# First x of an attention kernel loaded plainly and turned on TensorE, a smaller first piece of wq, and 40 instead of 48 heads with k turned on TensorE

## The chip, the core and the metric

The kernel runs on one core of a Trainium2 chip. The time is the device time of one execution in microseconds (us). Executions of one kernel differ here, so every comparison below is between several executions of both kernels made in the same rounds on the same chip, except where a single execution is named as such.

## The reference

Two independent problems, A and B, have the same shapes; the result is the two outputs side by side. Everything is bf16.

```python
# B=16 batches, Sq=144, D=448, H=16 heads, Sk=512 cached keys, Dh=256
q = (x @ wq).reshape(B, Sq, H, Dh).transpose(0, 2, 1, 3)
scores = einsum("bhqd,bhkd->bhqk", q, k_cache) * Dh ** -0.5
p = softmax(scores)
o = einsum("bhqk,bhkd->bhqd", p, v_cache)
out = o.transpose(0, 2, 1, 3).reshape(B, Sq, H * Dh) @ wo      # for A and for B
```

## The kernel before

One *unit* is one head of one batch: 256 units in A (numbers 0 to 255), 256 in B (256 to 511). Unit U needs its 256 columns of q, its k transposed (kT) and its v.

TensorE (PE) runs one step per unit. In step i it computes Q of unit i+3, the scores S of unit i+2, the product PV and the ones-sum (the row sums of the softmax, by a matmul with ones) of unit i, and some pieces of the output projection OP that are ready. kT comes in one of two ways. For the first units k is loaded plainly ("natural") and turned by 8 transposes on PE, which cost PE time. For the rest the load itself transposes, which costs PE nothing but holds the DMA queue about 1.6 times as long for each byte (17.07 us for the 4.2 MB of `k3` below, 1.35 us for a plain 512 KB).

All loads are issued by SyncE (SP) on one queue, in an order that is written down as a string for the start of A (START) and for the passage from A to B (MID). The letters are: `n3` plain k of units 6 and 7 (512 KB), `v3` their v (512 KB), `q0` a part of wq, `o0` an eighth of wo (448 KB), `x0` the x of four batches, transposed by the load in two issues, and `k3` a transposing load of the kT of 16 units, 48 to 63 (4.2 MB). `v` and `n` share a ring of nine slots; kT has room for 32 units.

```python
LQ, LS, LT = 3, 2, 4                 # Q, S and transposes run this many units ahead of PV
KW, KR = 16, 32                      # units per transposing load, units of kT kept
NV, NXG = 9, 2
NNAT = 3 * KW // UV                  # UV = 2 units per plain load: 24 loads, 48 units natural
# ...
START = ("n0 q0 x0 n1 v0 n2 q1 v1 n3 q2 n4 v2 n5 v3 q3 n6 v4 n7 v5 n8 v6 o0 n9 v7 n10 v8 o1 n11 v9 n12 v10 o2 n13 "
         "v11 n14 v12 o3 n15 v13 x1 n16 v14 o4 n17 v15 n18 v16 o5 n19 v17 n20 v18 o6 n21 v19 n22 v20 o7 n23 v21 v22 "
         "k3")
MID = ("k16 v127 v128 q0 v129 v130 q1 v131 q2 q3 v132 k17 v133 v134 v135 v136 v137 o0 o1 v138 o2 v139 o3 v140 o4 v141 "
       "o5 v142 o6 o7 k18")
# ...
def t_load_x(XG):                    # four batches of x, transposed by the load
    # ...
        q.dma_start_transpose(xt_sb[:, 0:3, c0:c0 + XB * SQ], x[:, 0:384]).then_inc(sems["xt%d" % sl], 16)
        return q.dma_start_transpose(xt_sb[:, 3, c0:c0 + XB * SQ], x[:, 320:448]).then_inc(sems["xt%d" % sl], 16)

def t_load_k(W):                     # kT of 16 units, transposed by the load
    # ...
        return q.dma_start_transpose(kt_sb[:, :, sl * KW * 128:(sl + 1) * KW * 128], src).then_inc(
            sems["kt%d" % sl], 16)

def t_tr(U, k):                      # half of a natural k: 4 transposes on PE, then a copy to kt_sb
    # ...
        for c in range(4):
            a = (4 * k + c) * 128
            ins = t.transpose(tr_ps[k][:, c * 128:(c + 1) * 128], v_sb[:, sl, j, a:a + 128], ident)

def q_pair(U):                       # 2: Q of this head for two batches at once, 1: for one, 0: done already
    b, h = unit(U)[1:]
    if U < NNAT * UV:
        return 1
    if U < NNAT * UV + H and h % 2 == 0:
        return 1
    # ... pairs from here on
# ... the program's steps, after the loads that are due in step i:
    u = i + LT
    if 0 <= u < NNAT * UV: t_tr(u, 0)
    u = i + LQ
    if 0 <= u < NT and q_pair(u): t_q(u); t_evac_q(u)
    u = i + LS
    if 0 <= u < NT: t_s(u)
    # ... t_tr(i + LT, 1), t_pv(i), t_sum(i), pieces of the output projection
```

## Time and profile before

| | before |
|---|---|
| time, median of the first 3 runs | 1067.63 us (1065.14 to 1068.06) |
| execution that was profiled | 1063.18 us, faster than all three |
| PE busy | 1043.1 of 1061.4 us |

In the profile, "PE" is the matmul unit, and a wait is idle time of an engine with the thing that ended it behind an arrow.

The page of before, three of its lines: the span, the busy time of the engines, and the chain of work that ended last by engine.

```profile
span 1061.4 us, 32383 instructions
...
PE 1043.1 (98%) x12736; PEld 895.5 (84%) x12736; DVE 670.9 (63%) x2063; ACT 706.4 (67%) x2133; POOL 625.6 (59%) x1030
...
PE 97%; DMA 2%; SPq 1%; DVE 0%; issue 0%; ACT 0%; DVEq 0%
```

PE is the bound: 97% of the chain is its own work. What is left to win is PE's work itself and some 18 us of idle time. The list of PE's waits of before says where most of that is; the columns are the total in us, how often, and the longest one.

```profile
PE s_ps L972 <- DMA v_sb<-in_A_k_cache_dram: 6.1, 4, 4.7
PE qp_ps L1018 <- DMA xt_sb<-in_A_x_dram: 3.6, 1, 3.6
PE ot_ps L1097 <- DMA v_sb<-in_B_v_cache_dram: 3.0, 1, 3.0
```

Two of the three are at the start of A: natural k (line 972 is the transposes) and x (line 1018 is Q); the third is in B. The timeline of SP of before shows why: start and duration of each issue, in us.

```profile
2.44 3.57 SPq L922 DMA_TRANSPOSE xt_sb<-in_A_x_dram  x1
6.05 1.87 SPq L923 DMA_TRANSPOSE xt_sb<-in_A_x_dram  x1
7.97 0.59 SPq L953 DMA_DIRECT2D v_sb<-in_A_k_cache_dram  x1
...
84.66 1.30 SPq L953 DMA_DIRECT2D v_sb<-in_A_k_cache_dram  x1
88.93 0.37 SPq L945 DMA_DIRECT2D v_sb<-in_A_v_cache_dram  x1
...
95.01 19.81 SPq L932 DMA_TRANSPOSE kt_sb<-in_A_k_cache_dram  x1
```

The two issues of x hold SP from 2.4 to 7.9 us, and the second natural k waits behind them. The last line is `k3`, the first transposing load of k: it takes SP 19.8 us to issue.

The timeline of PE of before, at the start and where `k3` is first used; the wait stands in brackets.

```profile
9.96 1.12 PE L1018 MATMUL qp_ps<-xt_sb,wq_sb 128*128 128x144 bf16 x8 [3.57 <-DMA xt_sb<-in_A_x_dram]
...
12.39 0.58 PE L972 MATMUL s_ps<-qt_sb,v_sb 128*128 128x128 bf16 x4 [0.88 <-DMA v_sb<-in_A_k_cache_dram]
...
119.93 0.66 PE L1052 MATMUL s_ps<-qt_sb,kt_sb 128*128 128x144 bf16 x8
120.43 0.66 PE L1097 MATMUL ot_ps<-pt_sb,v_sb 128*128 128x144 bf16 x8
```

The S at 119.93 is that of unit 48, the first to read `k3`. It has no bracket: `k3` had *landed* (its last byte had arrived) at 116.94 us (landings here and below are worked out from the traces), with 3.0 us to spare. Eight matmuls of 144 columns follow each other in 0.50 us at full rate (119.93 to 120.43), and take 0.96 us at half rate.

The table of stretches of before: stretch, length, busy time (and count) of PE, PEld, DVE, ACT and POOL, granted PE clock, DMA share, GB/s.

```profile
0.00:10.00 10.00, 1.66 (x13) 1.18 (x14) 2.67 (x4) 2.08 (x3) 0.70 (x6) 1.00 0.90 208
110.00:120.00 10.00, 10.00 (x137) 8.89 (x136) 6.81 (x26) 6.48 (x20) 5.48 (x10) 1.00 1.19 258
120.00:130.00 10.00, 10.00 (x127) 8.69 (x126) 6.75 (x20) 5.82 (x18) 5.00 (x9) 1.00 1.12 339
```

PE is nearly idle in the first ten microseconds and full around 120 us. But the queue has hardly a pause either: from 4.55 us to about 85 us, loads land one straight after another. There is one slack stretch, from about 85 to 98 us: SP waits there for PE to free a slot of `v` and `n` (nothing is issued between 85.96 and 88.93 us, see the timeline of SP), and landings come up to 2.6 us apart where 1.35 us is usual. The Trainium skill, "DMA: Bandwidth & Descriptors", section "Queues, rings and completion order", says that each DMA engine consumes descriptors in ring order; the trace agrees: in before all 86 transfers issued in the first 150 us land in the order of their issue.

### The profile page before, as it was taken

The numbers are of one execution on the slowest core, as the hardware profiler recorded it, in microseconds if no ns is written. First come the engines' busy times: TensorE is split into PE (matmuls) and PEld (weight loads), VectorE is DVE, ScalarE is ACT, GpSimd is POOL, SyncE is SP. The second block draws the span as 40 slices with busy tenths as digits, with TensorE's granted clock in tenths as the row PEclk, the third lists the DMA queues.
The fourth block names the chain that finished last, engine by engine and source line by source line (L and its number), as shares of the span: only waits on it lengthen the run. The fifth ranks groups of instructions, "written<-read, shape, count | busy, mean of one in ns | idle before, by whom it ended". The sixth has DMA issues, their size and how long they took to land.

```text
span 1061.4 us, 32383 instructions
## 1 busy us (share of the span) xinstructions
PE 1043.1 (98%) x12736; PEld 895.5 (84%) x12736; DVE 670.9 (63%) x2063; ACT 706.4 (67%) x2133; POOL 625.6 (59%) x1030
## 2 busy tenths in 40 slices
PE   6999999999999999999998999999999999999997
PEld 6999888888888888888887888888888888888885
DVE  4776666666666666666665666666666666666664
ACT  4887656667756666666855666676775666667674
POOL 3554555656656566666754656566665555666663
PEclk9999999999999999999998999999999999999999
DMA  9999999999999999999999999999999999999950
GB/s 304 379 350 285 295 293 254 274 297 273 292 276 298 208 280 267 290 292 298 262 287 352 265 274 290 291 290 301 264 263 265 304 285 289 289 290 279 239 187 13
DMA packets 588801, 294.15 MB, mean 277 GB/s; under 512 B 500576, under 2 KB 513376, under 8 KB 588640
## 3 DMA queue, kind: packets, MB, share of 16 engines
q1 hardware_dynamic: 588640, 291.99, 109.1%
q8 instruction: 102, 1.67, 0.6%
q14 instruction: 59, 0.48, 0.2%
HBM read 161.48 MB, written 4.13 MB: 156 GB/s over the span
## 4 chain that ended last, share of the span: by engine, by line
PE 97%; DMA 2%; SPq 1%; DVE 0%; issue 0%; ACT 0%; DVEq 0%
PE s_ps L1052 24%; PE ot_ps L1097 24%; PE qp_ps L1018 24%; PE op_ps L1196 20%; PE ot_ps L1109 3%; DMA v_sb<-in_A_k_cache_dram 1%; PE s_ps L972 1%; PE qp_ps L972 1%; PE qp_ps L1196 1%; DMA v_sb<-in_B_v_cache_dram 1%; SPq L922 0%; SPq L923 0%; DVE ost_sb L1217 0%; SPq L902 0%; DVE run_sb L1154 0%
## 5 line engine op out<-in xcount | busy, mean ns | idle before, releaser
L1072 POOL TENSOR_TENSOR pp_sb<-pt_sb 128x288 f32<-128x288 bf16 x512 | 374.0, 731 | 345.7 <-ACT pt_sb L1062 323.5
L1062 ACT ACTIVATE pt_sb<-s_ps 128x288 bf16<-128x288 f32 x1024 | 364.4, 408 | 268.5 <-PE s_ps L1052 268.0
L1154 DVE TENSOR_REDUCE run_sb<-ot_ps 1x1 bf16<-1x144 f32 x1024 | 262.3, 293 | 324.0 <-ACT rinv_sb L1120 324.0
L1097 PE MATMUL ot_ps<-pt_sb,v_sb 128*128 128x144 bf16 x4096 | 340.7, 226 | 3.0 <-DMA v_sb<-in_B_v_cache_dram 3.0
L1052 PE MATMUL s_ps<-qt_sb,kt_sb 128*128 128x144 bf16 x4096 | 340.8, 226 | 0.0
L1052 PEld LDWEIGHTS s_ps<-qt_sb,kt_sb 128*128 128x128 bf16 x4096 | 288.2, 98 | 43.5 <-DVE qt_sb L1032 0.2
L1018 PE MATMUL qp_ps<-xt_sb,wq_sb 128*128 128x288 bf16 (+1 forms) x2496 | 305.3, 266 | 3.6 <-DMA xt_sb<-in_A_x_dram 3.6
L1076 POOL TENSOR_TENSOR ps_sb<-pp_sb 128x144 bf16<-128x144 f32 x512 | 250.8, 490 | 76.2 <-PE ot_ps L1109 3.1
L1018 PEld LDWEIGHTS qp_ps<-xt_sb,wq_sb 128*128 128x128 bf16 x2496 | 218.8, 98 | 79.0 <-issue 4.4
L1196 PE MATMUL op_ps<-wo_sb,ring 128*128 128x448 bf16 x1120 | 285.0, 353 | 0.4 <-DVE ring L1140 0.4
L1097 PEld LDWEIGHTS ot_ps<-pt_sb,v_sb 128*128 128x128 bf16 x4096 | 274.6, 98 | 3.7 <-DMA v_sb<-in_B_v_cache_dram 3.2
L1140 DVE TENSOR_TENSOR ring<-ot_ps,rinv_sb 128x288 bf16<-128x288 f32 (+2 forms) x640 | 231.0, 375 | 0.0
L1120 ACT ACTIVATE rinv_sb<-ot_ps 128x144 f32<-128x144 f32 x512 | 150.1, 293 | 51.0 <-PE ot_ps L1109 8.0
L1032 DVE CAST qt_sb<-qp_ps 128x576 bf16<-128x576 f32 x200 | 151.1, 755 | 41.7 <-PE qp_ps L1018 37.6
L1125 ACT ACTIVATE rinv_sb<-rinv_sb 128x144 f32<-128x144 f32 x512 | 165.4, 323 | 16.1
L1109 PE MATMUL ot_ps<-ps_sb,ones 128*128 128x144 bf16 x512 | 115.9, 226 | 0.0
L1196 PEld LDWEIGHTS op_ps<-wo_sb,ring 128*128 128x128 bf16 x1120 | 94.0, 98 | 21.8 <-DVE ring L1140 0.8
L1031 DVE CAST qt_sb<-qp_ps 128x288 bf16<-128x288 f32 x112 | 49.2, 439 | 9.4 <-PE qp_ps L1018 8.8
L1109 PEld LDWEIGHTS ot_ps<-ps_sb,ones 128*128 128x128 bf16 x512 | 50.2, 98 | 0.0
L980 ACT ACTIVATE kt_sb<-qp_ps 128x512 bf16<-128x512 bf16 x48 | 28.9, 603 | 8.5 <-PE qp_ps L972 8.5
L972 PE MATMUL s_ps<-qt_sb,v_sb 128*128 128x128 bf16 x192 | 19.4, 226 | 6.2 <-DMA v_sb<-in_A_k_cache_dram 6.1
L980 DVE COPY kt_sb<-s_ps 128x512 bf16<-128x512 bf16 x48 | 19.5, 405 | 6.3 <-PE s_ps L972 6.2
(21 smaller groups left out, 85.1 us busy)
## 6 DMA issues: line engine op xcount, KB each, us to landing
v_sb<-in_A_v_cache_dram SPq DMA_DIRECT2D x128, 512.0 KB, 6.9
v_sb<-in_B_v_cache_dram SPq DMA_DIRECT2D x128, 512.0 KB, 7.1
v_sb<-in_A_k_cache_dram SPq DMA_DIRECT2D x24, 512.0 KB, 9.3
out_dram<-ost_sb SPq DMA_DIRECT2D x36, 112.0 KB, 6.1
wo_sb<-in_A_wo_dram SPq DMA_DIRECT2D x8, 448.0 KB, 8.5
wo_sb<-in_B_wo_dram SPq DMA_DIRECT2D x8, 448.0 KB, 8.9
wq_sb<-in_A_wq_dram SPq DMA_DIRECT2D x4, 768.0 KB, 9.2
wq_sb<-in_B_wq_dram SPq DMA_DIRECT2D x4, 768.0 KB, 10.1
```

Source lines behind the costliest of these rows:

```text
L1018: ins = t.matmul(acc, lhsT=wq_sb[:, kc, c0:c0 + 128], rhs=xt_sb[:, kc, xo:xo + n * SQ], start=(kc == 0), stop=(kc == 3))
L1032: return v.tensor_copy(qt_sb[:, a:b + 1:b - a, :, :], qp_ps[:, :, 0:2 * SQ].rearrange("p e (u q) -> p u e q", u=2))
L1052: ins = t.matmul(s_ps[bank][:, (c % 2) * SQ:(c % 2 + 1) * SQ], lhsT=kt_sb[:, 2 * c + dc, ko:ko + 128], rhs=qt_sb[:, qsl, dc, :], start=(dc ...
L1062: return a.activation(pt_sb[:, psl, 2 * k:2 * k + 2, :].rearrange("p b q -> p (b q)"), s_ps[bank][:, 0:2 * SQ], AF.Exp, scale=DH ** -0.5)
L1072: return g.tensor_tensor(pp_sb[:, :, :], pt_sb[:, psl, 0:2, :], pt_sb[:, psl, 2:4, :], op=ALU.add)
L1076: return g.tensor_tensor(ps_sb[:, sl, :], pp_sb[:, 0, :], pp_sb[:, 1, :], op=ALU.add)
L1097: ins = t.matmul(ot_ps[ob][:, dc * SQ:(dc + 1) * SQ], lhsT=v_sb[:, vsl, j, c * DH + dc * 128:c * DH + (dc + 1) * 128], rhs=pt_sb[:, sl, c, ...
L1109: return t.matmul(ot_ps[ob][:, 2 * SQ:3 * SQ], lhsT=ones[:, :], rhs=ps_sb[:, sl, :], start=True, stop=True)
L1125: return a.activation(rinv_sb[:, sl, :], ln, AF.Exp, scale=-1.0)
L1140: ins = v.tensor_tensor(ring[:, 2 * h:2 * h + 2, r0:r0 + q1 - q0], ot_ps[ob][:, 0:2 * SQ].rearrange("p (c q) -> p c q", c=2)[:, :, q0:q1], ...
L1154: return v.tensor_reduce(run_sb[0:1, k, j:j + 1], ot_ps[ob][0:1, 2 * SQ:3 * SQ], axis=AX.X, op=op)
L1196: ins = t.matmul(acc[0:m, 0:D], lhsT=ring[:, c, col0:col0 + m], rhs=wo_sb[:, c, :], start=(c == first), stop=(c == last))
```

## The change

The intent is to shorten the start and to take work off PE. x of batch 0 is loaded plainly and turned on PE, which waits there anyway. The first quarter of wq comes in two parts so that the first Q can start after one. The transposing `x0` (which still holds batch 0 to 3) is moved behind `v6`, and `x1` to the end. Units 40 to 47 no longer take 64 transposes on PE: a transposing load of 8 units (`k40.8`) brings their kT, and `k48.16` is the old `k3`.

```diff
-    NNAT = 3 * KW // UV
+    KO, Q1 = 8, 3
+    NNAT = 20
+    WQ_PARTS = (((0, 2), (2, 4)) + tuple((h, h + 4) for h in range(4, H, 4)), tuple((h, h + 4) for h in range(0, H, 4)))
@@
-    START = ("n0 q0 x0 n1 v0 n2 q1 v1 n3 q2 n4 v2 n5 v3 q3 n6 v4 n7 v5 n8 v6 o0 n9 v7 n10 v8 o1 n11 v9 n12 v10 o2 n13 "
-             "v11 n14 v12 o3 n15 v13 x1 n16 v14 o4 n17 v15 n18 v16 o5 n19 v17 n20 v18 o6 n21 v19 n22 v20 o7 n23 v21 v22 "
-             "k3")
+    START = ("n0 q0 n1 q1 v0 n2 q2 v1 n3 n4 v2 q3 n5 v3 n6 v4 q4 n7 v5 n8 v6 x0 n9 v7 n10 v8 o0 n11 v9 n12 v10 o1 n13 "
+             "v11 n14 v12 o2 n15 v13 o3 n16 v14 o4 n17 v15 n18 v16 o5 n19 v17 k40.8 v18 o6 v19 v20 o7 v21 v22 k48.16 v23 "
+             "v24 v25 x1")
@@ MID names its loads by first unit and count (k256.16 for k16), and is otherwise as before
@@
+        def t_load_xb():
+            def e(q):
+                q.dma_start(ost_sb[:, 0, :], A_x[0, 0:128, :]).then_inc(sems["xb"], 16)
+                return q.dma_start(ost_sb[0:SQ - 128, 1, :], A_x[0, 128:SQ, :]).then_inc(sems["xb"], 16)
+        def t_first_x():
+            def e(t):
+                for kc, d0 in enumerate((0, 128, 256, D - 128)):
+                    c0 = kc * SQ
+                    t.transpose(xb_ps[:, c0:c0 + 128], ost_sb[:, 0, d0:d0 + 128], ident)
+                    ins = t.transpose(xb_ps[:, c0 + 128:c0 + SQ], ost_sb[0:SQ - 128, 1, d0:d0 + 128], ...)
+            # then one DVE copy into the free second slot of xt_sb
@@ t_load_k(W) becomes t_load_k(u0, n): n = 8 or 16 units; two semaphores, one per 16 units of room
@@ def q_pair(U):
-            if U < NNAT * UV:
+            if b < Q1 and U < NU:
                 return 1
-            if U < NNAT * UV + H and h % 2 == 0:
+            if b == Q1 and U < NU and h % 2 == 0 and Q1 % 2:
                 return 1
@@
-            return 1 if j in (0, NXG * XB - 1) else (2 if j % 2 else 0)
+            if j in (0, NXG * XB - 1) or U // H in (XB - 1, XB):
+                return 1
+            return 2 if j % 2 else 0
```

Cut: the keys of wq and kT in the scheduler, and the parsing of the strings. The last part has a consequence: `x1` is now too late for pairs across batches 3 and 4, so the Q of units 49 to 63 are all single and those of 65 to 79 are no longer done ahead. There are 192 pairs and 128 single Q in place of 200 and 112.

More of the change, by code (lines that the diff above doesn't have):

```diff
@@ L806, in bass_concat_heads__mha_block_cached__gqa_block_cached__near_ridge_kernel @@
     LIM_EXP = 40
-    START = ("n0 q0 x0 n1 v0 n2 q1 v1 n3 q2 n4 v2 n5 v3 q3 n6 v4 n7 v5 n8 v6 o0 n9 v7 n10 v8 o1 n11 v9 n12 v10 o2 n13 "
-             "v11 n14 v12 o3 n15 v13 x1 n16 v14 o4 n17 v15 n18 v16 o5 n19 v17 n20 v18 o6 n21 v19 n22 v20 o7 n23 v21 v22 "
-             "k3")
-    MID = ("k16 v127 v128 q0 v129 v130 q1 v131 q2 q3 v132 k17 v133 v134 v135 v136 v137 o0 o1 v138 o2 v139 o3 v140 o4 v141 "
-           "o5 v142 o6 o7 k18")
+    START = ("n0 q0 n1 q1 v0 n2 q2 v1 n3 n4 v2 q3 n5 v3 n6 v4 q4 n7 v5 n8 v6 x0 n9 v7 n10 v8 o0 n11 v9 n12 v10 o1 n13 "
+             "v11 n14 v12 o2 n15 v13 o3 n16 v14 o4 n17 v15 n18 v16 o5 n19 v17 k40.8 v18 o6 v19 v20 o7 v21 v22 k48.16 v23 "
+             "v24 v25 x1")
+    MID = ("k256.16 v127 v128 q0 v129 v130 q1 v131 q2 q3 v132 k272.16 v133 v134 v135 v136 v137 o0 o1 v138 o2 v139 o3 v140 "
+           "o4 v141 o5 v142 o6 o7 k288.16")
     of = out.rearrange("b q e -> (b q) e")
@@ L847, in bass_concat_heads__mha_block_cached__gqa_block_cached__near_ridge_kernel @@
         tr_ps = (s_ps[2][:, :].bitcast(BF16), qp_ps[:, 1, :].bitcast(BF16))
+        xb_ps = op_ps[:, :].bitcast(BF16)
         ident = qt_sb[:, NQT - 1, 0, 0:128]
@@ L858, in bass_concat_heads__mha_block_cached__gqa_block_cached__near_ridge_kernel @@
             sem_names.append("xt%d" % i)
-        for i in range(HG):
+        for i in range(H // 2):
             sem_names.append("wq%d" % i)
+        sem_names.append("xb")
         for i in range(NWG):
@@ L893, in t_init, with t_load_wq @@
             S.add(POOL, e5, reads=[("ones", 0)], writes=[id_key], name="ident")
-        def t_load_wq(pr, hg):
-            cols = slice(hg * 4 * DH, (hg + 1) * 4 * DH)
+        def t_load_wq(pr, k):
+            h0, h1 = WQ_PARTS[pr][k]
+            cols = slice(h0 * DH, h1 * DH)
+            sem = "wq%d" % (h0 // 2)
             w = wqs[pr]
@@ L900, in e @@
                 q.dma_start(wq_sb[:, 0:3, cols], w[0:384, cols].rearrange("(c p) n -> p c n", p=128)).then_inc(
-                    sems["wq%d" % hg], 16)
-                return q.dma_start(wq_sb[64:128, 3, cols], w[384:448, cols]).then_inc(sems["wq%d" % hg], 16)
-            S.add(SP, e, writes=[(("wq", hg), pr)], dma_sem="wq%d" % hg, n_dma=2, name="wq%d.%d" % (pr, hg))
+                    sems[sem], 16)
+                return q.dma_start(wq_sb[64:128, 3, cols], w[384:448, cols]).then_inc(sems[sem], 16)
+            S.add(SP, e, writes=[(("wq", j), pr) for j in range(h0 // 2, h1 // 2)], dma_sem=sem, n_dma=2,
+                  name="wq%d.%d" % (pr, k))
         def t_load_wo(pr, wg):
@@ L924, in t_load_x, with ev, t_load_k @@
             S.add(SP, e, writes=[(("xt", sl), XG)], dma_sem="xt%d" % sl, n_dma=2, name="x%d" % XG)
-        def t_load_k(W):
-            pr, r0 = divmod(KW * W, NU)
-            sl = W % (KR // KW)
-            src = ks[pr].rearrange("b h (p c) d -> (b h p) (c d)", c=4)[r0 * 128:(r0 + KW) * 128, :]
+        def t_load_xb():
             def e(q):
-                return q.dma_start_transpose(kt_sb[:, :, sl * KW * 128:(sl + 1) * KW * 128], src).then_inc(
-                    sems["kt%d" % sl], 16)
-            S.add(SP, e, writes=[(("kt", sl), W)], dma_sem="kt%d" % sl, name="k%d" % W)
+                q.dma_start(ost_sb[:, 0, :], A_x[0, 0:128, :]).then_inc(sems["xb"], 16)
+                return q.dma_start(ost_sb[0:SQ - 128, 1, :], A_x[0, 128:SQ, :]).then_inc(sems["xb"], 16)
+            S.add(SP, e, writes=[(("ost", 0), -1), (("ost", 1), -1)], dma_sem="xb", n_dma=2, name="xb")
+        def t_first_x():
+            def e(t):
+                ins = None
+                for kc, d0 in enumerate((0, 128, 256, D - 128)):
+                    c0 = kc * SQ
+                    t.transpose(xb_ps[:, c0:c0 + 128], ost_sb[:, 0, d0:d0 + 128], ident)
+                    ins = t.transpose(xb_ps[:, c0 + 128:c0 + SQ], ost_sb[0:SQ - 128, 1, d0:d0 + 128],
+                                      ident[0:SQ - 128, 0:SQ - 128])
+                return ins
+            S.add(PE, e, reads=[(("ost", 0), -1), (("ost", 1), -1), id_key], writes=[("opp", "x")], banks=["op"],
+                  name="TX")
+            def ev(v):
+                return v.tensor_copy(xt_sb[:, :, XB * SQ:(XB + 1) * SQ],
+                                     xb_ps[:, 0:4 * SQ].rearrange("p (k q) -> p k q", k=4))
+            S.add(DVE, ev, reads=[("opp", "x")], writes=[(("xt", 1), -1)], banks=["op"], name="etx")
+        def t_load_k(u0, n):
+            pr, r0 = divmod(u0, NU)
+            c0 = u0 % KR * 128
+            sem = "kt%d" % (u0 % KR // KW)
+            src = ks[pr].rearrange("b h (p c) d -> (b h p) (c d)", c=4)[r0 * 128:(r0 + n) * 128, :]
+            def e(q):
+                return q.dma_start_transpose(kt_sb[:, :, c0:c0 + n * 128], src).then_inc(sems[sem], 16)
+            S.add(SP, e, writes=[(("kt", o % (KR // KO)), o) for o in range(u0 // KO, (u0 + n) // KO)], dma_sem=sem,
+                  name="k%d.%d" % (u0, n))
         def v_source(t, G):
@@ L959, in t_tr @@
             ko = U % KR * 128
-            kt_key = ("kt", U // KW % (KR // KW))
-            if k == 0 and U % KW == 0:
+            kt_key = ("kt", U // KO % (KR // KO))
+            if k == 0 and U % KO == 0:
                 S.res[kt_key] = _Res()
-                S.res[kt_key].version = U // KW
+                S.res[kt_key].version = U // KO
             bank, eng = (("s2", DVE), ("qp1", ACT))[k]
@@ L1008, in t_q @@
             xo = b % (NXG * XB) * SQ
-            xr = sorted(set((pr * Bn + b + k) // XB for k in range(n)))
-            hg = h // 4
+            xr = [(("xt", XG % NXG), XG) for XG in sorted(set((pr * Bn + b + k) // XB for k in range(n)))]
+            if U < H:
+                xo, xr = XB * SQ, [(("xt", 1), -1)]
             def e(t):
@@ L1020, in e @@
                 return ins
-            S.add(PE, e, reads=[(("wq", hg), pr), ("wqz", 0)] + [(("xt", XG % NXG), XG) for XG in xr],
+            S.add(PE, e, reads=[(("wq", h // 2), pr), ("wqz", 0)] + xr,
                   writes=[(bk, ("q", U)) for bk in q_banks[:n]], banks=q_banks[:n], name="Q%d" % U)
@@ L1038, in t_s @@
         def t_s(U):
-            W = U // KW
-            ksl = W % (KR // KW)
+            W = U // KO
+            ksl = W % (KR // KO)
             ko = U % KR * 128
@@ L1229, in bass_concat_heads__mha_block_cached__gqa_block_cached__near_ridge_kernel @@
         t_init()
+        t_load_xb()
+        t_first_x()
         s_min = -LQ - 24
@@ L1241, in bass_concat_heads__mha_block_cached__gqa_block_cached__near_ridge_kernel @@
             plan(lo, 0, t_load_x, XG)
-        for W in range(NNAT * UV // KW, NKW):
-            plan(KW * (W + 1) - KR - LS, 1, t_load_k, W)
+        for W in range(NKW):
+            plan(KW * (W + 1) - KR - LS, 1, t_load_k, KW * W, KW)
         table = {"x": t_load_x, "q": t_load_wq, "o": t_load_wo, "k": t_load_k, "n": t_load_n, "v": t_load_v}
-        start, mid = ([(table[w[0]], ((pr,) if w[0] in "qo" else ()) + (int(w[1:]),)) for w in tab.split()]
-                      for pr, tab in enumerate((START, MID)))
+        start, mid = ([(table[w[0]], ((pr,) if w[0] in "qo" else ()) + tuple(int(k) for k in w[1:].split(".") if k))
+                       for w in tab.split()] for pr, tab in enumerate((START, MID)))
         dma_plan = list(start)
+        k_first = sum(args[1] for fn, args in start if fn is t_load_k) + NNAT * UV
         for G in range(NVG):
@@ L1254, in bass_concat_heads__mha_block_cached__gqa_block_cached__near_ridge_kernel @@
                 dma_plan.extend(mid)
-            if (fn, args) in dma_plan:
+            if (fn, args) in dma_plan or fn is t_load_k and args[0] < k_first:
                 continue
@@ L1271, in bass_concat_heads__mha_block_cached__gqa_block_cached__near_ridge_kernel @@
             elif fn is t_load_k:
-                lo = KW * (args[0] + 1) - KR - LS
+                lo = sum(args) - KR - LS
             elif fn is t_load_x and args[0] >= NXG:
```

## The prediction

> **What bounds the kernel now.** TensorE: the page gives PE 1043.1 of 1061.4 us busy, the chain of waits 97% PE, and the busy table by 10 us stretches shows PE full from 40 us on. The loss lies at the start: PE is busy 1.66 us in 0-10 us. The list of waits has 4.7 us for the first natural k, 3.6 us for the transposing load of x, then 1 us for the second natural k, and the timeline shows matmul groups at half rate (8 in 0.96 us) until 16.4 us, then full rate (0.50 us). The queue's timeline says why: the two x transposes hold it from 2.44 to 7.92 us. The queue is the second bound: from 10 to 60 us it moves 362-388 GB/s. Landings, from the trace: 1.34 us for each 512 KB plain load, 3.2 us for a wq quarter, 17 us for a 16-unit transposing k load (4.2 MB, 246 GB/s; the Trainium skill, "DMA: Bandwidth & Descriptors", Latency and other measured facts, has 261 GB/s for one kernel: roughly agreed).
>
> **What the change does.**
> 1. x of batch 0 comes plainly (129 KB, two issues of 0.5 us) and is turned by 8 transposes on a cold PE that waits anyway; the first Q waits for half a quarter of wq. Estimates: first natural k lands at 5.6 us instead of 4.6, first Q at 7.3 instead of 9.96, second natural k at 8.6 instead of 12.3, that of unit 12 at 28.8 instead of 33.9.
> 2. The x transposes are deferred, not removed: behind v6 they cost the queue about 3.6 us. I put their landing at 42.3 us; unit 16's Q wants them at about 41.6. So the 5 us gained early shrinks to about 2.2 us: the start is bound by the queue's bytes, and those are nearly the same.
> 3. 8 natural units fewer: 64 transposes at 4 in 0.22 us, 3.6 us less PE work, all on the critical path. Against it 8 paired Q become 16 single ones: 0.98 against 2 x 0.50 us, 0.2 us more.
> 4. The k load for units 40-47 takes 8.5 us of queue where plain loads took 5.4; the second x group leaves this stretch. Estimate: the load for units 48-63 lands at about 113.5 us (116.9 before), while PE wants it at about 114 (119.93 before, 3.0 us to spare). A stall of 0-2 us, 0.4 expected. Later k loads in the first problem have 9 to 15 us to spare. The second problem and the tail do not change.
>
> Sum: -2.2 -3.6 +0.2 +0.4 = about -5.3 us, 0.5%.
>
> **Prediction: 1062.3 us** (from 1067.6), range 1057.5 to 1066. Faster by over 2%: 1%; within 2%: 98%; slower by over 2%: 1%.
>
> **What would show it.** Right: 320 natural transposes on PE, not 384; first Q at about 7 us, full rate from about 15 us; a new PE wait of about 1 us for the x transposes near 42 us; PE at 60 us only 2-3 us ahead of before; from 120 us on 5-6 us ahead, constant to the end. Wrong: a lead at 60 us of 5 us or more, or a wait of over 2 us on the transposing k load near 100-115 us, or waits at units 64-80.
>
> **What would make it wrong.** The half-quarter of wq with 1 KB rows may move slower; the clock may rise later, as PE waits more between groups; the x transposes may hide in the queue's backlog, giving 2-3 us more; the k load may come later and give the 3.6 us back; and executions spread by half of the effect (1065.1 to 1068.1).

## The result

| | before | after |
|---|---|---|
| runs of the comparison, median | 1066.6 us (4 runs) | 1067.99 us (1067.58 to 1068.65, 4 runs) |
| ratio of after to before | | 1.0014 (0.9996 to 1.0031) |
| profiled execution | 1063.18 us | 1067.58 us |

A ratio here and below is the mean time of one kernel's fast runs over that of the other's fast runs of the same rounds, so it is not quite the ratio of the medians quoted; the bracket is its 95% interval. The time is the same within 2%, and it lies above the range that was predicted. There was no gain at all.

The page of after, the same three lines.

```profile
span 1065.6 us, 32388 instructions
...
PE 1042.7 (98%) x12744; PEld 894.3 (84%) x12744; DVE 669.2 (63%) x2064; ACT 703.8 (66%) x2125; POOL 624.5 (59%) x1030
...
PE 93%; DMA 4%; SPq 3%; DVE 0%; issue 0%; ACT 0%; DVEq 0%
```

PE's own part of the chain fell from 97% to 93%. PE's count rises by 8 (64 transposes fewer, 8 for x, 64 because 8 pairs of Q became 16 single ones). Its busy time falls by only 0.4 us, though the trade should save about 3 us: part of the work ran slower, as will be seen. The list of PE's waits of after:

```profile
PE ot_ps L1132 <- DMA v_sb<-in_B_v_cache_dram: 4.8, 2, 2.9
PE op_ps L945 <- DMA ost_sb<-in_A_x_dram: 3.1, 1, 3.1
PE s_ps L1087 <- DMA kt_sb<-in_A_k_cache_dram: 2.9, 1, 2.9
PE s_ps L1004 <- DMA v_sb<-in_A_k_cache_dram: 2.2, 4, 0.9
...
PE qp_ps L1053 <- DMA wq_sb<-in_A_wq_dram: 1.1, 3, 0.4
PE ot_ps L1132 <- DMA v_sb<-in_A_v_cache_dram: 0.9, 1, 0.9
```

The wait of Q for x (3.6 us) is gone and that for natural k fell from 6.1 to 2.2 us. The 3.1 us of the second line are only the time until the plain x has landed, at the very start, and the 1.1 us are for parts of wq. The first line lies in B, to which experiments come back. Two waits in the middle of A are new: 2.9 us for a transposing load of k, and 0.9 us for a v. The timeline of SP of after:

```profile
28.85 9.27 SPq L929 DMA_TRANSPOSE xt_sb<-in_A_x_dram  x1
...
72.96 14.08 SPq L964 DMA_TRANSPOSE kt_sb<-in_A_k_cache_dram  x1
...
91.60 23.80 SPq L964 DMA_TRANSPOSE kt_sb<-in_A_k_cache_dram  x1
```

These are `x0`, `k40.8` and `k48.16`. The timeline of PE of after, at the start and around the new waits:

```profile
7.50 1.14 PE L1053 MATMUL qp_ps<-xt_sb,wq_sb 128*128 128x144 bf16 x8 [0.29 <-DMA wq_sb<-in_A_wq_dram]
...
9.52 0.59 PE L1004 MATMUL s_ps<-qt_sb,v_sb 128*128 128x128 bf16 x4 [0.46 <-DMA v_sb<-in_A_k_cache_dram]
...
114.51 0.66 PE L1053 MATMUL qp_ps<-xt_sb,wq_sb 128*128 128x144 bf16 x8
118.09 0.67 PE L1087 MATMUL s_ps<-qt_sb,kt_sb 128*128 128x144 bf16 x8 [2.92 <-DMA kt_sb<-in_A_k_cache_dram]
119.66 1.14 PE L1132 MATMUL ot_ps<-pt_sb,v_sb 128*128 128x144 bf16 x8 [0.89 <-DMA v_sb<-in_A_v_cache_dram]
120.59 0.33 PE L1144 MATMUL ot_ps<-ps_sb,ones 128*128 128x144 bf16 x1
120.71 1.70 PE L1231 MATMUL op_ps<-wo_sb,ring 128*128 128x448 bf16 x4
122.20 0.97 PE L1053 MATMUL qp_ps<-xt_sb,wq_sb 128*128 128x144 bf16 x8
123.01 0.66 PE L1087 MATMUL s_ps<-qt_sb,kt_sb 128*128 128x144 bf16 x8
```

PE has done its Q at 115.0 us, and waits until `k48.16` lands at 118.05. It runs one S, waits again for the v that landed behind `k48.16` at 119.61, and then does PV, the sum, four pieces of OP and much of a Q at about half rate: the PV takes 0.93 us to the next line, not 0.50. The stretch from the Q at 114.51 to the S at 123.01 is 8.50 us long. At full rate its work is Q 0.50, S 0.50, PV 0.50, sum 0.06, four pieces 0.76 and Q 0.50, that is 2.82 us, with durations of the same groups in before's timeline. So 5.68 us are lost: 3.8 in waits, 0.3 in the ends of the two groups before the waits (which the next group otherwise covers), and 1.5 in half-rate work (119.66 to 123.01 us, 3.35 us, for work that takes 1.82). The page counts the last two as busy.

The table of stretches of after:

```profile
0.00:10.00 10.00, 5.09 (x37) 3.74 (x38) 3.59 (x6) 2.68 (x4) 0.70 (x6) 1.00 0.75 247
110.00:120.00 10.00, 6.19 (x79) 5.12 (x77) 4.00 (x15) 3.98 (x12) 4.31 (x7) 0.97 1.23 258
120.00:130.00 10.00, 10.00 (x119) 8.56 (x118) 5.18 (x18) 5.30 (x16) 4.21 (x8) 0.86 1.14 313
```

In 110 to 120 us PE is busy for 6.19 us, and in 120 to 130 the clock is 0.86. The stretch from 120 to 130 looks full, but is not at full speed.

A *lead* makes this additive: by how much earlier than in the first profile of before the PV of a unit starts. Leads are worked out from the PE records of the traces, each of one execution, some of them on another chip.

| unit | 8 | 14 | 28 | 44 | 48 | 96 | 250 | 320 | 511 |
|---|---|---|---|---|---|---|---|---|---|
| start of its PV in before, us | 35.5 | 47.5 | 75.7 | 116.1 | 125.2 | 226.2 | 527.9 | 678.0 | 1050.5 |
| lead of after, us | 2.20 | 1.30 | 1.30 | 4.44 | -0.29 | -1.51 | -1.51 | -4.00 | -4.00 |

The start gains 1.30 us, the missing transposes 3.14, and between units 44 and 96 all of it and 1.5 us more is lost. (Read from 44 to 96 and not between: the other order of the Q alone moves the lead up and down by some 3 us there, as in half_wo below, where nothing waits: 6.06, 8.90 and 5.80 at units 44, 64 and 80.) Then nothing moves until B begins, where another 2.5 us go. The loss in A fits the ratio: +1.5 us is 0.14%. What B adds is against a lucky execution, as experiments show below.

### The profile page after: what moved, and what is told of

It reads as the page before. It is cut to its first block, busy times and chain, and to the rows that moved or that the text cites. A ratio compares the mean times of both kernels' runs of the same rounds, so it can differ in the third digit from the quotient of the medians.

```text
span 1065.6 us, 32388 instructions
## 1 busy us (share of the span) xinstructions
PE 1042.7 (98%) x12744; PEld 894.3 (84%) x12744; DVE 669.2 (63%) x2064; ACT 703.8 (66%) x2125; POOL 624.5 (59%) x1030
## 4 chain that ended last, share of the span: by engine, by line
PE 93%; DMA 4%; SPq 3%; DVE 0%; issue 0%; ACT 0%; DVEq 0%
PE ot_ps L1132 23%; PE s_ps L1087 23%; PE qp_ps L1053 23%; PE op_ps L1231 19%; PE ot_ps L1144 3%; SPq L964 2%; DMA wq_sb<-in_A_wq_dram 1%; DMA v_sb<-in_A_k_cache_dram 1%; DMA v_sb<-in_B_v_cache_dram 1%; PE s_ps L1004 1%; PE qp_ps L1004 1%; PE qp_ps L1231 1%; DMA v_sb<-in_A_v_cache_dram 0%; SPq L906 0%; SPq L977 0%
## 5 line engine op out<-in xcount | busy, mean ns | idle before, releaser
L1053 PEld LDWEIGHTS qp_ps<-xt_sb,wq_sb 128*128 128x128 bf16 x2560 | 222.4, 99 | 78.7 <-DVE qt_sb L1066 1.1
L1155 ACT ACTIVATE rinv_sb<-ot_ps 128x144 f32<-128x144 f32 x512 | 149.9, 293 | 54.9 <-PE ot_ps L1144 10.8
L1067 DVE CAST qt_sb<-qp_ps 128x576 bf16<-128x576 f32 x192 | 145.1, 756 | 40.3 <-PE qp_ps L1053 36.4
L1066 DVE CAST qt_sb<-qp_ps 128x288 bf16<-128x288 f32 x128 | 56.3, 440 | 8.2 <-PE qp_ps L1053 7.4
L1012 ACT ACTIVATE kt_sb<-qp_ps 128x512 bf16<-128x512 bf16 x40 | 24.1, 603 | 6.0 <-PE qp_ps L1004 6.0
L1249 ACT ACTIVATE ost_sb<-op_ps 128x448 bf16<-128x448 f32 x35 | 18.5, 530 | 2.4 <-PE op_ps L1231 2.3
L1012 DVE COPY kt_sb<-s_ps 128x512 bf16<-128x512 bf16 x40 | 16.2, 405 | 4.8 <-PE s_ps L1004 4.6
## 6 DMA issues: line engine op xcount, KB each, us to landing
wq_sb<-in_B_wq_dram SPq DMA_DIRECT2D x4, 768.0 KB, 10.8
```

The source lines that it names most:

```text
L1053: ins = t.matmul(acc, lhsT=wq_sb[:, kc, c0:c0 + 128], rhs=xt_sb[:, kc, xo:xo + n * SQ], start=(kc == 0), stop=(kc == 3))
L1155: return a.activation(ln, ot_ps[ob][:, 2 * SQ:3 * SQ], AF.Ln)
```

## The experiments

**Theory.** `k48.16` came 1.1 us later than `k3` had (118.05 against 116.94), and PE came to it 4.9 us earlier (115.0 against 119.93). The 3.0 us to spare became a wait of 3.0, the v behind it added one, the clock fell, and all that the change had gained was given back. **Rivals.** (1) The new start itself does harm later, through the late x, the late `x1` and the single Q. (2) Only the size of one load is at fault: in halves, its first half would come in time. (3) The queue simply has too many bytes to move by then, whatever the order. (4) The loss in B is a part of the effect.

The first four kernels ran together; before's median beside them was 1066.09 us.

### no_nat: the new start with 48 natural units

```diff
-    NNAT = 20
+    NNAT = 24
-  ... v17 k40.8 v18 o6 v19 v20 o7 v21 v22 k48.16 v23 v24 v25 x1
+  ... v17 n20 v18 o6 n21 v19 n22 v20 o7 n23 v21 v22 k48.16 v23 v24 v25 x1
```

> The change without its natural part: 48 units natural again (four plain k loads of 1.3 us each back in place of the 8-unit transposing k load), everything else of the change kept. Theory A (the lead is lost at one place: the 16-unit transposing k load for units 48-63 stands behind the 8-unit one in the queue and lands at 118.05 us, 3 us after PE wants it): here it lands at about 114 us, PE wants it at about 118.6, no wait on it, and the 1.3 us of lead that PE has at 45-75 us stay to the end of the first problem: about 1.2 us faster than before. Theory B (the first 150 us are bound by the queue's bytes as a whole, so any lead of PE is taken back at some later load): a wait of 1 us or more at a load after unit 48, time equal to before.

Measured: 1065.24 us (six runs, one of them 1070.6), ratio 1.0004 (0.9984 to 1.0024): the same as before. The lead is 1.35 us from unit 14 to 44, and `k48.16` lands at 115.77 with no wait on it. At 153 us PE waits 0.8 us for a v, and of the lead 0.14 us is left at unit 96. So the start part gains something by itself and loses it to the same queue 40 us later, in a smaller way; my expectation that the lead would stay was wrong, and the time is what its theory B said. Rival 1 is not needed for A: nothing here is worse than before.

### nat_only: the old start, 40 natural units

```diff
-  x of batch 0 loaded plainly and turned on PE; wq's first quarter in two parts
+  as before: START of before up to v17
-  ... v17 n20 v18 o6 n21 v19 n22 v20 o7 n23 v21 v22 k3
+  ... v17 k40.8 v18 o6 v19 v20 o7 v21 v22 k48.16
   # not undone: the single Q of units 49 to 79, as in after
```

> Only the natural part: x and wq loaded as before (x transposes first, second x group in its old place), 40 units natural, the 8-unit and the 16-unit transposing k loads in the queue. Theory A: lead 0 until unit 32, about 3.6 us by unit 44, then the load for units 48-63 lands at about 121 us while PE wants it at 116.4: a wait of about 4.5 us, and half-rate matmuls for some us after it, 6 to 7 us lost; about 3 us slower than before in all. Rival C (the loss in the changed kernel comes from the x part, for example the second x group behind that k load, not from the k loads): no wait at unit 48, about 3.5 us faster than before.

Measured: 1070.29 us, ratio 1.0039 (1.0022 to 1.0056), slower than before. `k48.16` lands at 120.16 us. The timeline of PE of nat_only, where it is first used:

```profile
120.21 1.14 PE L1085 MATMUL s_ps<-qt_sb,kt_sb 128*128 128x144 bf16 x8 [2.99 <-DMA kt_sb<-in_A_k_cache_dram]
122.33 1.14 PE L1130 MATMUL ot_ps<-pt_sb,v_sb 128*128 128x144 bf16 x8 [0.98 <-DMA v_sb<-in_A_v_cache_dram]
```

The same pair of waits, and half rate at once (1.14 us for a group that takes 0.66 at full rate). The lead rises by 3.3 us from unit 28 to 44, then falls by 7.1 us to unit 96 (2.40 to -4.69). Taking the natural transposes away therefore makes the loss by itself, but for the single Q that this kernel still shares with after, worth 0.25 us (half_wo below). This is the theory's strongest evidence against rival 1.

### split_k48: the load for units 48 to 63 in two halves

```diff
-  ... v22 k48.16 v23 v24 v25 x1
+  ... v22 k48.8 v23 v24 k56.8 v25 x1
-        for i in range(KR // KW): sem_names.append("kt%d" % i)
+        for i in range(KR // KO): sem_names.append("kt%d" % i)
```

> The changed kernel with one thing more: the transposing k load for units 48-63 goes out as two of 8 units, with two v loads between them (four semaphores for kt instead of two). The bytes are the same and their order nearly so. Theory A: the first half lands at about 109.5 us, PE wants it at about 115: no wait at unit 48, no fall of the clock, lead of about 4.4 us at unit 46 kept (about 4.2 us at the end of the first problem instead of -1.5), so about 5.7 us faster than the changed kernel, about 4 us faster than before, if the second problem does not change. Theory B: a wait of 3 us or more at unit 56, or at units 64-80, and the time of the changed kernel (within 1 us).

Measured: 1068.53 us, ratio 1.0026 (1.001 to 1.0041): no better than after. The halves land at 109.66 and 122.81 us, there is no wait on them, and the lead is 4.7 us at unit 48. Then comes the next transposing load, `k64.16`, at 153.28 us. The timeline of PE of split_k48 there:

```profile
153.33 1.14 PE L1087 MATMUL s_ps<-qt_sb,kt_sb 128*128 128x144 bf16 x8 [3.71 <-DMA kt_sb<-in_A_k_cache_dram]
154.83 1.14 PE L1132 MATMUL ot_ps<-pt_sb,v_sb 128*128 128x144 bf16 x8 [0.36 <-DMA v_sb<-in_A_v_cache_dram]
```

The wait has moved from unit 48 to unit 64 and grown, and the clock falls again. At unit 96 the lead is -3.76 us. Before had 8.9 us to spare at unit 64 (landing 147.31, use 156.22); here `k64.16` lands 6.0 us later. So rival 2 is wrong for one load alone, and my expectation with it: the queue is behind until after unit 64, and a 16-unit load anywhere in that time is a trap.

### split_k_both: the same, and two more 16-unit loads of B in halves

```diff
-    MID = ("... v132 k272.16 v133 v134 v135 ... o6 o7 k288.16")
+    MID = ("... v132 k272.8 v133 v134 k280.8 v135 ... o6 o7 k288.8 v143 v144 k296.8")
```

> As the one before, and in the second problem the k loads for units 272-287 and 288-303 also go out in halves, with v loads between. In the traces of both kernels PE waits about 3 us at unit 266 on a v load that stands behind a 16-unit k load, and the changed one waits again at unit 286 on k and v. Theory A (one large transposing load that blocks the queue is the cause there too): both waits go, 3 to 8 us more than the run with the first split alone, so 7 to 12 us faster than before. Theory B (the queue's bytes bound the start of the second problem): the waits move to later loads and the time is that of the run before within 1.5 us.

Measured: 1066.87 us, ratio 1.0016 (1.0 to 1.0031). In A the lead is -2.13 us at unit 96. At the start of B it rises by 6.0 us against the profile of before (from -2.13 to 3.89 at unit 270), then falls to -1.25 by unit 320. I had expected 7 to 12 us less than before; it is not faster. B has a tight stretch of its own, and there too a split in one place moves the wait on.

The next four ran together on another chip; before's median beside them was 1066.28 us.

### half_wo: half of A's wo not loaded (wrong result)

```diff
+            n = WOG if pr else WOG // 2
-                return q.dma_start(wo_sb[:, c0:c0 + WOG, :], ...)
+                return q.dma_start(wo_sb[:, c0:c0 + n, :], ...)    # the other half is set to zero once by POOL
```

> Wrong result on purpose: the changed kernel, but only half of each wo load of the first problem is made (the other half of the tile is set to zero once by GpSimd), so the queue carries about 4.8 us less before unit 48 and TensorE's work is the same. Splitting the k load did not help: the wait went from unit 48 to unit 64, with no pause in the queue's landings. Theory B (queue bytes as a whole bind the first 150 us): with 4.8 us fewer the k load for units 48-63 lands at about 113.3 us, that for 64-79 at about 146.5, PE waits for neither, the lead at unit 96 is about +4 us instead of -1.5, and the time is about 5.5 us under the changed kernel (1062.5) if the second problem stays as it is. Theory A (order in the queue, not bytes): no gain at unit 64 beyond 1 us.

Measured: 1060.87 us, ratio 0.9952 (0.9936 to 0.9968); the result is wrong, as meant. The order of the loads is that of after; eight loads are half as long, an estimated 4.8 us less of queue (half of 1.2 us each, from their landings). `k48.16` lands at 111.34 and `k64.16` at 144.40 us. The table of stretches of half_wo:

```profile
110.00:120.00 10.00, 10.00 (x139) 8.90 (x137) 6.23 (x24) 6.60 (x20) 5.85 (x10) 1.00 1.04 298
120.00:130.00 10.00, 10.00 (x135) 8.72 (x133) 6.30 (x21) 7.18 (x21) 6.03 (x11) 1.00 1.15 308
```

PE is full and the clock 1.00. The lead is 6.06 us at unit 44 and still 5.80 at units 96 and 250. This shows that the arrival of loads, not PE's work or the change of the Q, is what costs: with earlier loads the same PE program keeps its gain. The different pairing of Q costs at most the 0.25 us between units 44 and 80. (`k48.16` came 6.7 us earlier than in after, more than the estimated 4.8.) It also says that bytes matter, which favours rival 3; only an order with all the bytes can tell.

### k8_first, k8_both and k8_both_nat48: all transposing loads in pieces of 8 units

```diff
# k8_first
-  ... v22 k48.16 v23 v24 v25 x1
+  ... v22 k48.8 v23 v24 k56.8 v25 x1 v26 v27 v28 v29 v30 k64.8
-        for W in range(NKW):
-            plan(KW * (W + 1) - KR - LS, 1, t_load_k, KW * W, KW)
+        for W in range(NT // KO):
+            plan(KO * W - 18, 1, t_load_k, KO * W, KO)        # later loads too, each as late as 18 units ahead
# k8_both: also
-    MID = ("k256.16 v127 v128 q0 ... k272.16 ... k288.16")
+    MID = ("k256.8 v127 v128 q0 v129 v130 k264.8 q1 ... k272.8 ... k280.8 ... k288.8")
# k8_both_nat48: also NNAT = 24 and n20 to n23 in place of k40.8
```

> The changed kernel with every transposing k load of the first problem sent in pieces of 8 units, each ahead of four v loads, so that a load reaches the queue about 16 units before its use and none stands in front of something needed sooner; the second problem's start as it was. Bytes the same. If order is the cause after all (theory A in a finer form: there are enough bytes by each deadline, wrongly ordered): no wait at units 48, 56, 64, 72 or 80, lead at unit 96 about +4 us, time about 1062. If the bytes bind (theory B): waits of 3 us or more in all somewhere before unit 96, lead there 1 us or less.

> As the one before, and the start of the second problem also in pieces of 8 units, ordered by when each load is wanted (the wq quarters and v loads before the next k piece, wo later). Theory A: the waits at units 266 to 304 of the second problem go too, about 5 us more than the run before: about 1057. Theory B: waits of the same sum come later in the second problem; time within 1.5 us of the run before.

> As the one before, with 48 units natural as in the kernel before. Four plain loads of 1.35 us for one transposing load of 9.3 us: 3.9 us less queue time before unit 48, 3.6 us more TensorE time. Theory A: about 3 us slower than the run before (the natural units cost PE time on its critical path). Theory B: the same as the run before or faster, as the queue binds there.

Measured: 1076.65 us, ratio 1.0095 (1.0067 to 1.0122); 1073.59 us, 1.005 (1.0025 to 1.0074); 1071.3 us, 1.0043 (1.0024 to 1.0063). All three are slower than before, and my expectations for them were wrong. But A did what was wanted: in k8_first the lead is 5.12 us at unit 44 and 3.79 at units 96 and 250. The loss is in one place in the passage to B. The timeline of PE of k8_first there:

```profile
537.48 2.08 PE L1053 MATMUL qp_ps<-xt_sb,wq_sb 128*128 128x288 bf16 x8 [8.92 <-issue]
```

It is the first Q with B's wq. The profile names no releaser, but the trace has the landing of B's first wq part at 537.39 us, 0.09 us before that Q; in before it lands at 532.03. My late-as-possible plan put a piece of k at 491.99 and the 16-unit `k256.16` at 506.30 just ahead of it. The other two lose their lead at the same place, between units 250 and 257 (10.9 and 9.9 us, against 10.8 in k8_first), though B's first k comes in pieces of 8 there. So these three are badly built experiments for the question, and a lesson: the order of the whole queue counts, and here making loads late cost more than making one too big (5.7 us in after).

The last timed four ran together; before's median beside them was 1065.38 us.

### a96_first: 8-unit pieces for units 48 to 95 only, the rest as in after

```diff
-  ... v22 k48.16 v23 v24 v25 x1
+  ... v22 k48.8 v23 v24 k56.8 v25 x1 v26 v27 v28 v29 v30 k64.8 v31 v32 v33 v34 k72.8 v35 v36 v37 v38 x2 k80.8 v39 v40 v41 v42 k88.8
```

> The changed kernel with the transposing k loads of units 48 to 95 in 8-unit pieces in deadline order, all later loads as in the changed kernel. Theory A (order): no waits between units 46 and 96, lead at unit 96 about 4 us and held to unit 250 (no loss at unit 257, as the plan there is the old one), the second problem as in the changed kernel (a loss of about 2.5 us), time about 1062.5, that is 5 us under the changed kernel and 3 to 4 us under the one before. Theory B (bytes): a wait on the first 16-unit load after the pieces (unit 96 or 112), lead 1 us or less at unit 128.

Measured: 1062.56 us (1060.68 to 1064.31), ratio 0.9969 (0.9954 to 0.9985): faster than before by 0.31%, with all bytes of after and the right result. The pieces land at 109.21, 122.32, 143.55 and 158.43 us. The table of stretches of a96_first:

```profile
110.00:120.00 10.00, 10.00 (x135) 8.72 (x133) 6.23 (x25) 6.17 (x20) 5.90 (x10) 1.00 1.21 283
...
150.00:160.00 10.00, 10.00 (x120) 8.32 (x118) 6.19 (x20) 6.41 (x20) 5.46 (x9) 1.00 1.12 277
```

PE is full at clock 1.00 in both places where it had waited. There is no wait of PE between 105 and 165 us in its list. The lead is 4.18 us at unit 44, and 3.16 at units 96 and 250. So rival 3 is wrong as it stands: the bytes fit. (Nor is it the pieces alone that gain: best_nat48 below has them with 48 natural units, and a lead of only 0.47 at unit 96.) What after lacked was an order in which no load of 17 us stands between a unit and its v or k while the queue has nothing to spare.

### best: the same, and B's first transposing loads in pieces too

```diff
-    MID = ("... v132 k272.16 v133 v134 v135 ... o6 o7 k288.16")
+    MID = ("... v132 k272.8 v133 v134 k280.8 v135 ... o6 o7 k288.8 v143 v144 k296.8 v145 ... v150 k304.8 v151 v152 x5 k312.8")
```

> As the one before, and in the second problem the k loads for units 272 to 319 in 8-unit pieces with v loads between, the second x group there behind the load for 304. Theory A: no waits of more than 1 us at units 266, 286 and 304; the lead of 4 us becomes about 8 to 10 us; time about 1057. Theory B: the waits come back at units 320 to 352 and the time is that of a96_first within 1.5 us.

Measured: 1060.85 us (1058.25 to 1063.05), ratio 0.996 (0.9942 to 0.9977). This beats both kernels. The lead is 2.72 us at unit 250, 8.75 at 286 and 5.81 at 320. I had expected 8 to 10 us and a time of 1057: most of what B gave is taken back after unit 304 (4.09 is left at the end).

### best_nat48 and old_b: which part of best does what

```diff
# best_nat48: best with
-    NNAT = 20        ... v17 k40.8 v18 o6 v19 v20 o7 v21 v22 k48.8 ...
+    NNAT = 24        ... v17 n20 v18 o6 n21 v19 n22 v20 o7 n23 v21 v22 k48.8 ...
# old_b: before, with MID of best and nothing else
```

> As best, with 48 units natural as before the change (x still plain first). If the natural part pays once the order is right: 3 us slower than best. If its queue time takes back what it saves on PE: the same within 1 us.

> The kernel before (x transposed by the queue at the start, 48 units natural, 16-unit pieces in the first problem), with only the second problem's k loads for units 272 to 319 in pieces as in best. Theory A: the wait at unit 266 goes, about 4 to 5 us faster than before (1061.5), and best is faster than this by the 4 us that the change is worth in the first problem.

Measured: best_nat48 1066.9 us, ratio 1.0023 (1.0005 to 1.0042); old_b 1062.85 us, 0.9975 (0.9961 to 0.999). Best against best_nat48, in the same rounds, would be the worth of the fewer natural units with everything else in order: 6 us, where I had expected 3. That is more than the 3.6 us of PE's work; the lead of best_nat48 at unit 96 is only 2.3 us smaller (0.47 against 2.72), and the rest differs in B (-2.31 against 4.09 at the end). Why B differs I did not settle, so the 6 us are not shown to be the natural units'. The splitting in B alone is worth 0.25%, without any of the change; so best owes a part to it (it is 2.0 us under old_b, where I had expected 4), and a96_first is the kernel that shows what the change can give.

### before_again and after_again: one look each, on the same chip

before_again is after with every part of the change undone (the instructions of every engine are in the order of before); after_again is after unchanged. They tell how much of the traces repeats.

> The kernel before, built from the changed source with every part of the change undone (each engine's instructions are in the same order as in before). A second profile of it. If the first profile of before was a lucky execution in the second problem: about the same times as the first up to unit 250 (within 1 us, no wait at unit 48), and 2 to 3 us later from unit 290 on. If not: within 1 us everywhere.

> The changed kernel once more. The wait on the k load for units 48-63 is there again, 2 us or more, and 5 to 6 us of lead are lost between units 45 and 80, so at unit 96 it is 0.5 to 2.5 us behind the kernel before. Waits near units 266 and 286 to 304 of the second problem again, of sizes that vary by 1 to 3 us.

Measured: 1064.7 and 1070.28 us, single runs of unknown state; before beside them 1067.63. The wait on `k48.16` repeats in after_again (3.0 us, and 1.6 us for the v behind it), with a deeper fall of the clock. The table of stretches of after_again:

```profile
120.00:130.00 10.00, 8.93 (x86) 7.67 (x87) 3.69 (x14) 3.58 (x12) 3.64 (x6) 0.68 1.18 278
```

The leads at unit 96 are 0.37 and -3.97 us, so A costs 4.3 us in this pair and 1.5 us in the first. In B, from unit 250 to the end, before_again loses 1.8 us against the first profile of before and after_again 2.8 (after: 2.5; a96_first 3.35; half_wo 1.3). By these two the first profile of before was a quick one in B. Rival 4 falls for the most part: of the 2.5 us that after seemed to lose there, 1.0 us remains in this pair (2.8 less 1.8), and two single looks do not show even that to be the change's.

## Why the prediction was wrong

Prediction and measurement, in the terms of the sum (the measured terms are from the leads of after):

| term | predicted, us | measured, us |
|---|---|---|
| start | -2.2 | -1.3 |
| natural transposes of 8 units | -3.6 | -3.1 |
| fewer pairs of Q | +0.2 | +0.25 |
| wait for the k of units 48 to 63, with what follows | +0.4 | +5.7 |
| sum | -5.3 | +1.5 |

1. **The start.** The size came out near, but not for the reason given. The first natural k was predicted at 5.6 us and landed at 5.43; the first Q at 7.3 and started at 7.50; full rate about 15 us, found at 13.63. The second natural k came at 9.4 us, not 8.6. x of the first group was predicted to land at 42.3 us and to make PE wait about 1 us; it landed at 41.58 and nothing waited, as the Q of unit 16 came only at 42.67. So it was not this wait that shrank the early gain: the lead was 2.79 us at unit 0 and down to 1.63 by unit 12, in short waits such as 0.67 us for a natural k at 19.20 and 0.42 us for wq at 26.04. The lead at 60 us was to be 2 to 3 us and was 1.30. Over the twelve traces with the new start the lead at unit 14 has a mean of 1.1 us (-0.0 to 2.5), over the four with the old start -0.3, so the start is worth about 1.4 us.

2. **The natural transposes.** Right: 320 are left, and the lead rises by 3.1 us over the units concerned. nat_only, with 3.3 us, shows it by itself.

3. **The Q.** Right: half_wo bounds it at 0.25 us.

4. **The k load for units 48 to 63: the step that failed.** The prediction had it landing at about 113.5 us with PE wanting it at about 114, a stall of 0 to 2 us, 0.4 expected. PE wanted it at 115.0, near enough. The load landed at 118.05, 4.5 us later than predicted. The landings in the two traces add up as follows.

| step of the queue's time | us |
|---|---|
| landing of `k3` in before | 116.94 |
| `x1` no longer ahead of it (its two landings in before, 1.49 and 2.12) | -3.61 |
| up to `v17` otherwise (82.34 less 3.61 in before, 80.61 in after) | +1.88 |
| from `v17` to `v22` (17.53 in before, 19.82 in after) | +2.29 |
| the load itself (17.07 in before, 17.62 in after) | +0.55 |
| landing of `k48.16` in after | 118.05 |

The prediction had 3.6 us for `x1` and 3.1 us for `k40.8` (8.5 against 5.4), which makes 116.4 us of 116.94. To come to 113.5 it must have carried another 2.9 us of gain in the queue; the record does not say from where, and the only one that it names is that of the start. That is the mis-sized term: measured, the queue was not 2.9 us ahead of before at `v17`, once `x1` is taken out, but 1.9 us behind. no_nat and nat_only bear this out one by one: no_nat, with the new start, has `v17` at 80.82, as in after (80.61), and its `k48.16` comes only 1.17 us before `k3` had and not 6.5 (2.9 and 3.6); nat_only, with the old start, has `k48.16` 3.22 us later than `k3`, near the predicted 3.1. The early gain was mostly one of order: the k of unit 12 landed at 29.75, 4.16 us before that of before (5.1 predicted), but before had loaded the last quarter of wq (3.2 us) ahead of it and after had not. At the next k, with that quarter loaded in both, the difference was 1.03 us (35.58 against 36.61), and `x0` was still to come in after. In before the x transposes stand at the very start and take about 3.0 us of landings there (from wq's last byte at 7.95 to the natural k at 12.26, less 1.34 for that k). In after they stand in the middle of a stream without a pause and take 3.8 us (from 39.51 to 44.66, less 1.35), and with the plain x ahead of it the first natural k lands 0.9 us later than before. (From `v17` to `v22` after's queue took only 2.29 us longer, as before's has its slack stretch there, with landings 2.60, 2.53 and 1.81 us apart.) PE was ahead, and its supply was behind. The prediction did say that the transposes "are deferred, not removed", and among its risks that "the k load may come later and give the 3.6 us back", but it drew the consequence for PE at 60 us and not for the load at 118.

The second mistake is of the cost of a wait. The prediction took a stall of a microsecond for a microsecond. The 2.9 us brought a second wait of 0.9 us, as the v stood behind the load, and 1.5 us lost to work at half rate. The Trainium skill, "TensorE: Matmul & The Clock Gate", Part 1, says that the clock halves after an idle window of about 3.4 us that runs freely, and takes as much busy time to come back, so that it varies from run to run. The traces agree as to size and variability: by the clock records of the traces the half rate lasted from 119.42 us for 3.41 us in after (0.86 in the stretch above), and from 119.61 us for 6.83 us, twice as long, in after_again (0.68). The prediction used the clock only for the start.

The test that the prediction set itself did its work: "a wait of over 2 us on the transposing k load near 100-115 us, or waits at units 64-80" was named as the sign of being wrong. The first came, at 115.2 to 118.1 us, just after the stretch named. split_k48 shows the second, after the first is taken away: the 9 to 15 us that later k loads were said to have to spare were those of before, and at unit 64 after had only 2.8 us left of 8.9 (landing 151.31, use 154.12).

5. **"The second problem and the tail do not change."** Not contradicted: the traces differ there by up to 2.5 us, but the repeats of both kernels scatter by as much.

**What is shown and what is not.** That late loads eat the gain is shown by half_wo (fewer bytes, gain kept) and a96_first (same bytes, other order, most of the gain kept and a time of 1062.56 us, about what was predicted for after). That the removal of the natural transposes makes the loss without the new start is shown by nat_only (but for the 0.25 us of the single Q). The sum of the queue's landings is arithmetic on two traces; no run moved `x0` alone, so how the 1.9 us at `v17` divide between `x0`, the plain x and the smaller pieces of wq is not shown. Why the passage to B varies by 1 to 3 us between executions is open, as is why best_nat48 does so much worse in B than best.

## What to carry to other kernels

When a change takes work from the busiest engine near the start, compare it load by load with the queue: a consumer that comes 5 us earlier to a load with 3 us to spare has gained 3 us at most, and a long load just ahead of it can take back more than that through the loads behind it and the clock. Moving a slow transfer out of the way moves its cost to every later load until the queue first has a pause, so carry the sum forward to there, and not only to the next use (that it ends at a pause is argued, not tested here). In this kernel it paid to split long transposing loads while the queue was tight, all of them up to the first with time to spare; splitting one only moved the wait to the next (split_k48).

## What the Trainium skill lacked or had wrong

- "DMA: Bandwidth & Descriptors", Latency and other measured facts, has 261 GB/s for transposing loads in one kernel. Here 4.2 MB took 16.9 to 17.9 us in the first 150 us, 234 to 248 GB/s, and pieces of half the size 8.4 to 9.7 us (after, split_k48). It gives nothing on the load behind one: after the 8-unit piece `k40.8` the second landing came after 2.71 us, not 1.2, and the one after `x0` after 3.08, not 1.35.
- Same page, "Issuing engines are not separate DMA queues", calls the issuing time of a sequencer "usually small relative to the DMA itself". For transposing loads it was not short here: issuing 16 units held SP for 19.8 us in before and 23.8 us in after, against some 17 us between landings, and the first of the two issues of `x0` for 9.3 us in after. Whether SP works in that time or waits for room in the queue, no run shows.
- "TensorE: Matmul & The Clock Gate", Part 1, does not say how busy a window may be and still count as idle. Here the clock fell after waits of 2.99 us (nat_only) and of 2.92 and 0.89 us with one group between them (after); PE had been busy for 0.88 and 0.67 us of the 3.41 us before the fall, and at one fall in B for 1.49 us (after_again, 614.54 us).
- No page says how large the scatter of a long kernel is: the same program took 1063.2 to 1069.9 us in all runs of before, over four sets of rounds, and its traces differ by 1.8 us in B alone.
